# Linear attention and a mixture of experts on one core: 32-row inverses on GpSimd, and another order of the recurrence

## The chip, the core and the metric

One core of a Trainium2 chip runs the whole program in one launch. It has five engines with a queue each: PE (TensorE, matmuls), DVE (VectorE), ACT (ScalarE), POOL (GpSimd) and SP (SyncE, which only issues DMAs here). An engine takes its instructions in the order in which they were written and waits at each for what that one needs. The metric is the time of one execution in microseconds of the device, as the median of several runs.

## What is computed

The reference has three parts in a row, and all of it counts:

```
for t in range(768):                       # for each of 4 batches and 8 heads, state is 40x40
    y[t]  = r[t] @ state
    Sa    = state @ a[t]
    state = state * w[t] - outer(Sa, b[t]) + outer(v[t], k[t])
x   = rows of y, 3072 x 320
moe1: 8 experts, each row goes to its best one:  x = gate * (relu(x @ w1[e]) @ w2[e])
moe2: soft experts on 32 slots:  softmax over rows (dispatch) and over slots (combine)
```

## The kernel before, in words

**The attention stage** cuts the 768 steps into six chunks of 128. A chunk of one batch is a unit: 24 units, numbered u = 4 * chunk + batch, each with its 8 heads as four pairs. Within a unit the recurrence is turned into matmuls. The decays are multiplied up along the time axis by scans (P from the end, Q from the start); at L182 and bk at L174 and L184 are the inputs scaled by them; L206 and L223 form the lower triangles that say how a step acts on later ones (tiles lab and LAK). The 32 x 32 blocks on lab's diagonal have to be inverted, 32 heads and batches of a chunk and four blocks each. SP's DMAs gather them into the tile LD (gen_q); gen_t transposes LD on DVE (L257) so that each partition holds whole blocks, inverts two 16 x 16 halves by substitution, 15 steps of a product (L268) and a subtraction (L269), on DVE in chunk 0 and on POOL after that, and transposes back (L272, L275). gen_y then puts in the remaining 16 x 16 corner for each unit: 32 small matmuls (L284), an ACT copy (L287), 32 more (L292), a DVE subtraction (L295). gen_m uses the inverses: the two matmul groups L339 solve a unit's 128 rows in steps of 32, units k and k-1 together, with matmuls of zeros (L301) between. gen_a forms the outputs and the next state, gen_z turns them for the route and the next chunk. The route picks experts, scales the rows xt (L542, POOL) and scatters them by indirect DMA.

**The MoE stage** begins when the attention stage's banks are free, and keeps PE busy with L688, L706 and their like.

**The order** is written by hand. Each generator (d and c loads, e decays, k, b, q, x, t, y, m, a, z, r, and i and f for the initial memsets and the zero fills of two DRAM tables, issued on ACT's queue at L1189 and L1192) yields after a step, and the string SCHED (L1209) says by one letter at a time which generator takes its next step. Every engine's queue follows from it. PSUM has six banks in rotation (`bank`, L118) and two for gen_m. Weights for the MoE and the rest come by SP's queue.

The functions that the change touches:

Of the kernel before, what the change touches and what calls it, by code (L numbers as in the profile page):

```python
# [18 lines left out]
T = 128  # L19
NT = S // T  # L20
NP = 4
# [28 lines left out]


def blocks(a, o, dims):
    return bass.AP(a.tensor, a.offset + o, [list(a.ap[0]), [528, 2]] + dims)
# [16 lines left out]
def stage_attn(ctx, tc, la_d, vp_d, rz_d, vt_d, cst, rt):  # L70
# [19 lines left out]
    GB = [t[:, 0:H * (64 + D)].rearrange("t (h c) -> t h c", h=H) for t in gb_]  # L90
    GS = [per.tile([T, H, 32], F32, name=f"GS{i}") for i in range(2)]
    LAK = per.tile([T, H, T], F32, name="LAK")
# [10 lines left out]
    def load_first():  # L103
        pair = [RP, 2, NP, T]
        std = [pin.tile([RP, NP, T], F32, name=n, bufs=1 if i else 2) for i, n in enumerate(("lw", "lb", "la", "lk"))]
        lw1 = pin.tile([RP, NP, T], F32, name="lw", bufs=2)
        ba1, ba2 = (pt.tile(pair, F32, name="Tt", bufs=2) for x in range(2))
        ks = [t[:, 0:NP * T].rearrange("r (p t) -> r p t", p=NP) for t in gb_]
# [46 lines left out]
    def gen_e(u):  # L155
        lw = LA[u][0]
        At = AT[u] = pk.tile([RP, NP, T], F32, name="At", bufs=7)
        nc.scalar.activation(At, lw, AF.Relu, bias=lim[:, 0:1], scale=-1.0, accum_out=wf[:, 2 * u:2 * u + 1])
        nc.scalar.activation(At, lw, AF.Relu, bias=lim[:, 1:2], scale=1.0, accum_out=wf[:, 2 * u + 1:2 * u + 2])
        yield  # L160
        P = PT[u] = pk.tile([RP, NP, T + 1], F32, name="P", bufs=2)
        Q = QT[u] = pk.tile([RP, NP, T + 1], F32, name="Q", bufs=8)
        w = WE[u] = pk.tile([RP, NP, 1], F32, name="wend", bufs=10)
        nc.vector.memset(P[:, :, T:T + 1], 1.0)
        nc.vector.tensor_scalar(lw, lw, WLO, WHI, ALU.max, ALU.min)
        yield
        for p in range(NP):
            nc.vector.tensor_tensor_scan(rev(P[:, p, 0:T]), rev(lw[:, p, :]), one, 1.0, ALU.mult, ALU.mult)
            if p == 1:
                yield  # L170
        nc.vector.reciprocal(Q[:, :, 0:1], P[:, :, 0:1])  # L171
        yield
        bk = BK[u] = pl.tile([RP, NP, 2 * T], F32, name="bk", bufs=2)
        nc.gpsimd.tensor_tensor(ends(bk), LA[u][1].rearrange("r p (i s) -> r p i s", i=2),  # L174
                                P[:, :, 1:T + 1].rearrange("r p (i s) -> r p i s", i=2), ALU.mult)
        nc.gpsimd.tensor_copy(w, P[:, :, 0:1])
        yield
        for p in range(NP):
            nc.vector.tensor_tensor_scan(Q[:, p, 1:T + 1], lw[:, p, :], one, Q[:, p, 0:1], ALU.mult, ALU.mult)  # L179
            if p % 2:  # L180
                yield
        (nc.vector if u in (1, 3) else nc.gpsimd).tensor_tensor(At, LA[u][2], Q[:, :, 0:T], ALU.mult)  # L182
        yield
        nc.gpsimd.tensor_tensor(bk[:, :, 64:64 + T], LA[u][3], P[:, :, 1:T + 1], ALU.mult)  # L184
        yield

# [13 lines left out]
    def gen_b(u):  # L200
# [6 lines left out]
        yield  # L207
        lab = LAB[u] = pk.tile([T, H, T], F32, name="lab", bufs=7)
        if u == 0:
# [21 lines left out]
    def gen_q(u):  # L231
        tt, b = divmod(u, B)
        if b == 0:
            LD[tt] = pt.tile([T, B * H, 32], F32, name="Ld")
        for c in range(4):
            o = 32 * c
            nc.sync.dma_start(out=LD[tt][o:o + 32, b * H:(b + 1) * H, :], in_=LAB[u][o:o + 32, :, o:o + 32])
        yield
# [16 lines left out]
    def gen_t(tt):  # L255
        M = pt.tile([T, 32, 32], F32, name="Tm")
        nc.vector.transpose(out=M, in_=LD[tt].rearrange("p h t -> p t h"))  # L257
        yield
        eng = nc.gpsimd if tt else nc.vector
        eng.memset(blocks(VI, 0, [[32, 16], [1, 16]]), 0.0)  # L260
        eng.memset(blocks(VI, 0, [[33, 16]]), 1.0)
        tmp = pt.tile([T, 128], F32, name="Tx")
        yield
        for s in range(15):
            n, m = 15 - s, s + 1
            w = tmp[:, 0:2 * n * m].rearrange("p (k n m) -> p k n m", k=2, n=n)
            v = blocks(VI, 32 * (s + 1), [[32, n], [1, m]])
            eng.tensor_tensor(w, blocks(M, 33 * s + 32, [[32, n], [0, m]]), blocks(VI, 32 * s, [[0, n], [1, m]]), ALU.mult)  # L268
            eng.tensor_tensor(v, v, w, ALU.subtract)  # L269
            yield  # L270
        R = TT[tt] = pt.tile([T, B * H, 32], F32, name="Tt", bufs=2)
        nc.vector.transpose(out=R.rearrange("j h t -> j t h"), in_=VI)  # L272
        yield
        W = DT[tt] = pt.tile([T, B * H, 16], F32, name="Dt", bufs=1)
        nc.vector.transpose(out=W.rearrange("j h s -> j s h"), in_=VI[:, :, 0:16].rearrange("j t s -> j s t"))  # L275
        yield

    def gen_y(u):
        tt, b = divmod(u, B)
        R, gs = TT[tt][:, b * H:(b + 1) * H, :], GS[u % 2]  # L280
        ps = bank(T, H, 16)
# [165 lines left out]
    def gen_i():  # L447
# [10 lines left out]
        for i in range(2):  # L458
            nc.gpsimd.memset(GS[i], 0.0)
            nc.gpsimd.memset(RI[i][:, :, T:T + D], 0.0)  # L460
            for o in (0, 64):
                nc.gpsimd.tensor_copy(RI[i][o:o + D, :, T:T + D], eye[o:o + D, None, o:o + D].to_broadcast([D, NP, D]))
            yield
# [11 lines left out]
    def units(f, lo=0, by=1):  # L475
        for u in range(lo, U, by):
            yield from f(u)

    def routes():
        for tt in range(NT - 1):  # L480
# [3 lines left out]

    streams = dict(d=units(gen_d, B), c=units(gen_c), e=units(gen_e), k=units(gen_k), b=units(gen_b), q=units(gen_q),
                   x=units(gen_x), y=units(gen_y), m=(y for k in range(U + 1) for y in gen_m(k)), a=units(gen_a), z=units(gen_z),
                   t=(y for tt in range(NT) for y in gen_t(tt)), r=routes(), i=gen_i(), f=gen_f(), w=gen_w())
    load_first()
    for c in cst["sched"]:
        next(streams[c], None)  # L490
    for c in "idcekbqxtymazrf":
        for _ in streams[c]:
            pass


class Route:
# [9 lines left out]
    def run(self, tt, lg, xt, pp, tag, b0=0, b1=B):  # L506
# [34 lines left out]
        V.reciprocal(sm, sm)  # L541
        nc.gpsimd.tensor_tensor(xt[:, :, 1:XW], xt[:, :, 1:XW], sm.to_broadcast([T, n, DM]), ALU.mult)  # L542
        V.tensor_copy(xt[:, :, 0:1], cst["idm"][:, ti, None])
# [606 lines left out]
def program(tc, a, out_d):  # L1150
# [58 lines left out]
SCHED = (  # L1209
    "iicciieeiieieieeeffffdedidmmieeeeebbdeeeekecbbbbkkcbbkeekbkkbkebqbbxbebebxddebxbbbebbebqbxmeeebxxekebebbbekkkb"  # L1210
    "bbebbbqbxeeeebxexekbeebbkkdbbbbekebbbqbxeeeddddbxtxkbtbbbtbkktbbbbtbqbxkttttxtxttttttttteyeyyeeyydemyeymeeedmb"
    "dddmymebebkbemmbbbedkbemebbbqbeeedxdddmbexxembbbbkbmybeebmkemydbbeybqbxmeydmxbxdddmmabmaaabbbbmaaabaamebeccmbk"
    "amyamabkbqbeymaaamttcmaktmaztmaeztzatxaztzkaztxztxamazaaattmaccatamttytaaatyteecmtdkmmakkmazktzzzzmzyzemyzyemm"
    "ayeeedmmddadabeambebmaaekaaybmabbdbebmkccayaabbbqbexaeaaxxedeecbdddmbaazbbkzzmybbzzembzyzkebmmzeaebmabadabqbex"
    "aaeaaaxmxedacceaaedddmbaaabebbcbbbbaazbbmzezbqkmbzzxzmzkmzxkmykeemxykmedymakyemaaaerdemedddbaakabyamabbbemkacc"
    "yaambmbbaaabbbqbcmaazmzzttmzzxmzmztaextzmxataatmtaaaatamtyacctaayttmataamtmtctmatazemkzztmzdzkkmztzmakzmaeaaey"
    "aameyaaameedeyccbdddakabaybbbekbmbebaemamabbdbqbecxaazexmzzxemkzzmkzedzeeybdddmkbzebrmmmyakyaakkabbbaabaaamyba"
    "cacabebebqbedxeaeaaxxedeecbdddmbaazbbmyzezbbkzzebzbmeezybmzkbdybqbxmyemxxkmeymarkemdyaraaeedddbmbaayaaabbbmbka"
    "ccmbaaymembramababmbqbcmakazmezzxzttezmazzxdmazataexttmetaaktaaamktmacctaamtmtmataatmtctmatazmtzzetzzzrzmadmaa"
    "ameezaaaaacacbddadatbbbbbbbmaaabbbqbecexayaxzexkyzzeeyzzkkydzemkzymezmmyreedeybdddkbmmybbbbymebbmaebmkbeamaebq"  # L1220
    "aybdmxeaamexaaaxermdkamccyaeadddekbyaaabebbbbcbbaazbbmzezbqkzebzxmzekzdmxzxekmymaekrmaaaedymeedddbyaabaakabbmb"
    "bmacbcaamymebaaabbbqbcmakazmzzmezzttexmzmzadxzmxtaeaattemtaatkaaamktmatccaatmmtmtaaatmtctmataztmzzetzzrzzdmama"
    "aameezaaaaaabccadddatbbbbbybmabayaebbbqbecxeyaexazxymzedzmkezzyzzmerkkmzykerdyembydddembebkbymbbbbemabbekmeaam"
    "bqbayedxmaaeaaaxxdmeaccaamdmdeebkbmabaakbbbbmcebaazbbmzezbqmkebzzxezmzakemxazaaermxeaaaaambaccaabbbbbbbaaabbbq"
    "bckayakzymzttzmyzzmktzztmyzktymtkymtktrmxmamxaaaxmtaaaaatmtmrccataammtrmaaamcmaazmtzzzztztzmazttmaaamtaayaaamy"
    "yaccaaymaaammcmaazmzzmzzzyzmzmaymaaamaaaaamyaccaaymaaammcmaazzzmzzmzzzmymarymaaamaaaaamyaccaaymaammcmazzzmrzmz"
    "ymmaymazaarmaaaaaryaccaamymaammcmazzzmzmzzmmamaaamaaaaammaccaammaammazzzzzzmaraaaraaaaaaaarraaazzzzzzrrrr"
)
# [74 lines left out]
```

## Time and profile before

| | |
|---|---|
| time, median of 3 runs | 893.78 us (891.35 to 899.17) |
| the profiled execution | 880.59 us, of which the span is 878.6 us |
| PE / DVE / ACT / POOL busy | 780.0 / 483.9 / 363.4 / 234.0 us |
| first matmul of the MoE stage | 588 us |
| first use of a chunk's inverse, chunks 1 to 5 (L339) | 157.7, 232.8, 324.6, 409.7, 503.6 us |

The profile is one execution. Busy time is the time in which an engine works; waits are named by what ended them (`<-`). PEclk is the clock that TensorE was granted, as a share of full speed. Line numbers with an L are lines of the kernel above. The profiled execution is the fastest of those known of this kernel.

### The profile page before, as it was taken

What the parts mean: (1) busy time and instruction counts of PE and PEld (TensorE: products, weight loads), DVE (VectorE), ACT (ScalarE), POOL (GpSimd) and SP (SyncE); (2) the same over time, 40 slices, a digit from 0 to 9 for tenths busy, and PEclk for the clock granted to TensorE, in tenths of its full rate; (3) what the DMA queues carried; (4) which work ended last, traced back from release to release, by engine and by line L of the source; (5) the groups of instructions that cost most, each with busy time, mean ns of one, the idle gap of its engine ahead of it and who ended that gap; (6) DMA issues with size and microseconds to landing.
All of it is one profiled execution on the core that took longest, in us unless ns stands there. A gap on an engine that the chain in (4) does not pass through costs nothing. (4 is left out here: it accounts for less than half of the span.)

```text
span 878.6 us, 31034 instructions
## 1 busy us (share of the span) xinstructions
PE 780.0 (89%) x13468; PEld 661.4 (75%) x13468; DVE 483.9 (55%) x1334; ACT 363.4 (41%) x898; POOL 234.0 (27%) x404
## 2 busy tenths in 40 slices
PE   1385999999998987998999999979999999999894
PEld 1274888888877876887888687749999999999532
DVE  4378654665664674655373334355567666665423
ACT  1363553564653454544353131324444444443122
POOL 7131325223433543263225202020022012201210
PEclk9995598899996998998596798989999999999697
DMA  8822433443442343424231213345665567545755
GB/s 303 250 46 59 120 103 89 110 124 82 116 142 94 84 122 96 127 67 138 78 71 36 61 47 84 100 123 146 183 185 153 148 189 197 157 148 184 275 168 184
DMA packets 140627, 113.94 MB, mean 130 GB/s; under 512 B 64004, under 2 KB 118564, under 8 KB 140484
## 3 DMA queue, kind: packets, MB, share of 16 engines
q1 hardware_dynamic: 134304, 102.28, 41.2%
q10 hardware_dynamic: 3956, 5.09, 1.9%
q0 software_dynamic: 2224, 4.51, 1.5%
q8 instruction: 108, 1.77, 0.8%
q14 instruction: 35, 0.29, 0.1%
HBM read 95.73 MB, written 12.97 MB: 124 GB/s over the span
## 5 line engine op out<-in xcount | busy, mean ns | idle before, releaser
L784 POOL DMA_INDIRECT c_d<-cn,ix x32 | 34.2, 1068 | 218.0 <-DVE cn L781 202.1
L688 PE MATMUL psh<-xh,w1h 128*128 128x416 f32 x192 | 71.8, 374 | 0.0
L301 PE MATMUL psr<-zero 32*32 32x192 f32 x552 | 65.8, 356 | 2.2 <-issue 1.8
L690 ACT ACTIVATE hh<-psh 128x416 fp32r<-128x416 f32 x64 | 33.2, 519 | 81.5 <-PE psh L688 80.4
L174 POOL TENSOR_TENSOR bk<-lb,P 128x512 f32<-128x512 f32 x21 | 24.8, 1183 | 155.7 <-DVE Q L171 44.5
L692 DVE SCALAR_TENSOR_TENSOR hl<-psh,hh 128x416 fp32r<-128x416 f32 x64 | 37.8, 590 | 37.0 <-ACT hh L690 37.0
L344 ACT ACTIVATE GA<-psr 32x320 f32<-32x320 f32 x48 | 20.5, 428 | 85.2 <-PE psr L339 84.1
L328 PE MATMUL psr<-GA,lab 32*32 32x40 f32 (+1 forms) x768 | 51.8, 224 | 0.5 <-issue 0.5
L339 PE MATMUL psr<-Rs,Tt 32*32 32x40 f32 x1536 | 48.6, 214 | 1.7 <-issue 1.6
L395 PE MATMUL ps<-GA,KB 128*40 128x168 f32 (+1 forms) x384 | 48.2, 329 | 0.2 <-issue 0.2
L328 PEld LDWEIGHTS psr<-GA,lab 32*32 32x32 f32 (+1 forms) x768 | 45.2, 132 | 3.0 <-issue 1.0
L179 DVE TENSOR_TENSOR_SCAN Q<-lw,Q,one 128x128 f32<-128x128 f32 x88 | 47.1, 586 | 0.4
L706 PE MATMUL pso<-hh,w2h 128*128 128x416 f32 x128 | 45.4, 355 | 0.0
L206 PE MATMUL ps<-At,bk 64*128 64x128 f32 x384 | 38.3, 349 | 8.0 <-POOL bk L184 8.0
L688 PE MATMUL psh<-xl,w1h 128*128 128x416 f32 x128 | 45.3, 354 | 0.0
L688 PE MATMUL psh<-xh,w1l 128*128 128x416 f32 x128 | 45.1, 353 | 0.0
L707 PE MATMUL pso<-hh,w2l 128*128 128x416 f32 x128 | 44.8, 350 | 0.0
L398 DVE TENSOR_TENSOR yT<-ps,Q 104x256 f32<-104x256 f32 x48 | 20.2, 421 | 44.7 <-PE ps L395 44.3
L708 PE MATMUL pso<-hl,w2h 128*128 128x416 f32 x128 | 44.7, 350 | 0.0
L339 PEld LDWEIGHTS psr<-Rs,Tt 32*32 32x32 f32 x1536 | 41.6, 119 | 3.0 <-issue 2.8
L193 PE MATMUL ps<-kmask,bk 104*128 104x104 f32 x192 | 30.4, 295 | 15.1 <-ACT LAK L217 15.1
L212 ACT COPY lab<-ps 64x512 f32<-64x512 f32 x48 | 25.9, 580 | 43.4 <-PE ps L206 38.0
(272 smaller groups left out, 2114.8 us busy)
## 6 DMA issues: line engine op xcount, KB each, us to landing
r<-in_w SPq DMA_DIRECT2D x32, 320.0 KB
p<-in_p SPq DMA_DIRECT2D x16, 640.0 KB
r<-in_w SPq DMA_DIRECT2D x32, 256.0 KB
p<-in_p SPq DMA_DIRECT2D x8, 1024.0 KB
RI<-in_rz SPq DMA_DIRECT2D x24, 256.0 KB
vs<-in_vp SPq DMA_DIRECT2D x24, 256.0 KB
lw<-in_la SPq DMA_DIRECT2D x22, 256.0 KB
lb<-in_la SPq DMA_DIRECT2D x21, 256.0 KB
```

Of the source, the lines that this page charges most:

```text
L179: nc.vector.tensor_tensor_scan(Q[:, p, 1:T + 1], lw[:, p, :], one, Q[:, p, 0:1], ALU.mult, ALU.mult)
L206: nc.tensor.matmul(low[x][:, p, :], lhsT=bk[o:o + KP, p, 0:T], rhs=At[o:o + KP, p, :], start=True, stop=True)
L301: nc.tensor.matmul(bk[o:o + 32, DM:512], lhsT=z[i:i + 32, 0:32], rhs=z[i:i + 32, 0:512 - DM], start=False, stop=True, skip_group_check=Tru ...
L328: nc.tensor.matmul(R[o:o + n, h, :], lhsT=LAB[u][r:r + n, h, o:o + n], rhs=val(u, r // 32)[r:r + n, h, :], start=False, stop=True, skip_gr ...
L339: nc.tensor.matmul(R[o:o + 32, h, :], lhsT=TT[u // B][o:o + 32, u % B * H + h, :], rhs=Rs[o:o + 32, h, :], start=True, stop=True, skip_gro ...
L395: nc.tensor.matmul(ps[o:o + D, i, j:w], lhsT=KB[u][j // 64][:, 2 * p + x, :], rhs=G[:, 2 * p + x, :], start=False, stop=True, skip_group_c ...
L688: nc.tensor.matmul(ps, lhsT=l, rhs=r, start=(i == 0), stop=(i == len(ops) - 1))
L692: V.scalar_tensor_tensor(hl, ps, 0.0, hh.bitcast(F32), ALU.max, ALU.subtract)
L706: nc.tensor.matmul(o, lhsT=wh[:, c], rhs=hh, start=(f == 0), stop=False)
L707: nc.tensor.matmul(o, lhsT=wl[:, c], rhs=hh, start=False, stop=False)
L708: nc.tensor.matmul(o, lhsT=wh[:, c], rhs=hl, start=False, stop=(f == NF - 1))
L784: q = nc.gpsimd.indirect_dma_start(out=c_d[:], out_offset=bass.IndirectOffsetOnAxis(ap=ix[:, j:j + 1], axis=0), in_=cn[:, j, :], in_offset ...
```

## The change

Five things are different.

- The inverse of chunks 1 to 5 is one 32 x 32 substitution on POOL, 31 steps of a product (L289 after the change) and a subtraction (L290); gen_y is left for the four units of chunk 0. The result goes back into LD, which has two buffers, and the tile DT is there for chunk 0 only.
- The clamped decays are written to a PSUM bank (wc) and not over lw, and both kinds of scans read them there.
- The three products on POOL are a stream of their own, p; the copy of wend goes to ACT. At and lab have a buffer more.
- The scaling of xt in the route is four ACT instructions in place of one on POOL.
- SCHED is another string: the fills, the initial memsets and all the rest stand elsewhere.

```diff
+def diag(a):
+    ap = [list(x) for x in a.ap]
+    return bass.AP(a.tensor, a.offset, [ap[0], [33, 32]])
...
     def gen_e(u):
         lw = LA[u][0]
-        At = AT[u] = pk.tile([RP, NP, T], F32, name="At", bufs=7)
+        At = AT[u] = pk.tile([RP, NP, T], F32, name="At", bufs=8)
...
-        nc.vector.tensor_scalar(lw, lw, WLO, WHI, ALU.max, ALU.min)
+        wc = bank(RP, NP, T)
+        nc.vector.tensor_scalar(wc, lw, WLO, WHI, ALU.max, ALU.min)
         yield
         for p in range(NP):
-            nc.vector.tensor_tensor_scan(rev(P[:, p, 0:T]), rev(lw[:, p, :]), one, 1.0, ALU.mult, ALU.mult)
+            nc.vector.tensor_tensor_scan(rev(P[:, p, 0:T]), rev(wc[:, p, :]), one, 1.0, ALU.mult, ALU.mult)
...
+        for p in range(NP):
+            nc.vector.tensor_tensor_scan(Q[:, p, 1:T + 1], wc[:, p, :], one, Q[:, p, 0:1], ALU.mult, ALU.mult)
+            if p % 2:
+                yield
+
+    def gen_p(u):
+        P, At = PT[u], AT[u]
         bk = BK[u] = pl.tile([RP, NP, 2 * T], F32, name="bk", bufs=2)
         nc.gpsimd.tensor_tensor(ends(bk), LA[u][1].rearrange("r p (i s) -> r p i s", i=2),
                                 P[:, :, 1:T + 1].rearrange("r p (i s) -> r p i s", i=2), ALU.mult)
-        nc.gpsimd.tensor_copy(w, P[:, :, 0:1])
-        yield
...
+        nc.scalar.copy(WE[u], P[:, :, 0:1])
         yield
         nc.gpsimd.tensor_tensor(bk[:, :, 64:64 + T], LA[u][3], P[:, :, 1:T + 1], ALU.mult)
+        yield
+        (nc.vector if u in (1, 3) else nc.gpsimd).tensor_tensor(At, LA[u][2], QT[u][:, :, 0:T], ALU.mult)
...
         M = pt.tile([T, 32, 32], F32, name="Tm")
         nc.vector.transpose(out=M, in_=LD[tt].rearrange("p h t -> p t h"))
         yield
...
+        else:
+            nc.gpsimd.memset(VI, 0.0)
+            nc.gpsimd.memset(diag(VI), 1.0)
+            tmp = pt.tile([T, 512], F32, name="Tx")
+            yield
+            for s in range(31):
+                n, m = 31 - s, s + 1
+                w = tmp[:, 0:n * m].rearrange("p (n m) -> p n m", n=n)
+                v = VI[:, s + 1:32, 0:m]
+                nc.gpsimd.tensor_tensor(w, M[:, s + 1:32, s:s + 1].to_broadcast([T, n, m]), VI[:, s:s + 1, 0:m].to_broadcast([T, n, m]), ALU.mult)
+                nc.gpsimd.tensor_tensor(v, v, w, ALU.subtract)
+                yield
+        R = TT[tt] = LD[tt]
         nc.vector.transpose(out=R.rearrange("j h t -> j t h"), in_=VI)
...
-        nc.gpsimd.tensor_tensor(xt[:, :, 1:XW], xt[:, :, 1:XW], sm.to_broadcast([T, n, DM]), ALU.mult)
+        for j in range(n):
+            nc.scalar.mul(xt[:, j, 1:XW], xt[:, j, 1:XW], sm[:, j])
...
-    "iicciieeiieieieeeffffdedidmmieeeeebbdeeeekecbbbbkkcbbkeekbkkbkebqbbxbebebxddebxbbbebbebqbxmeeebxxekebebbbekkkb"
+    "eecceeeeeedeieeieeiiiipdpeeepdippipikebefemebdcfkkbkbfkkbbbbkbbibqkbbexbefpxxdbbbbpebbebepbbqbbepexbbpdebbbbbk"
```

What the order does is seen in three places. The first is the head of ACT's queue: the limit checks of the units' decays, the zero fills (xs and c_d) and the first evictions. Before:

```order
L158 ACTIVATE At,wf<-lw,lim 128x512
L159 ACTIVATE At,wf<-lw,lim 128x512
L1189 DMA xs<-zero 104x8x321
L1192 DMA c_d<-zero 128x256
L1189 DMA xs<-zero 104x8x321
L1192 DMA c_d<-zero 128x256
L1189 DMA xs<-zero 104x8x321
L1192 DMA c_d<-zero 128x256
L1189 DMA xs<-zero 104x8x321
L158 ACTIVATE At,wf<-lw,lim 128x512
L159 ACTIVATE At,wf<-lw,lim 128x512
L212 COPY lab<-ps 64x4x128 x2
```

After:

```order
L163 ACTIVATE At,wf<-lw,lim 128x512
L164 ACTIVATE At,wf<-lw,lim 128x512
L163 ACTIVATE At,wf<-lw,lim 128x512
L164 ACTIVATE At,wf<-lw,lim 128x512
L163 ACTIVATE At,wf<-xt,lim 128x512
L164 ACTIVATE At,wf<-xt,lim 128x512
L189 COPY wend<-P 128x4 x2
L1215 DMA xs<-zero 104x8x321
L1218 DMA c_d<-zero 128x256
L163 ACTIVATE At,wf<-xt,lim 128x512
L164 ACTIVATE At,wf<-xt,lim 128x512
L221 COPY lab<-ps 64x4x128
```

All seven fills stood ahead of the second unit's check; now three units' checks stand ahead of the first two fills, and the others come one by one after evictions.

The second is POOL's queue in the inverse of chunk 2 (Tm holds the blocks, VI the inverse). Before:

```order
L174 TENSOR_TENSOR bk<-lb,P 128x4x2x64
L176 COPY wend<-P 128x4
L182 TENSOR_TENSOR At<-la,Q 128x512
L184 TENSOR_TENSOR bk<-lk,P 128x4x128
L260 MEMSET VI 128x2x16x16
L261 MEMSET VI 128x32
L268 TENSOR_TENSOR Tx<-Tm,VI 128x30
L269 TENSOR_TENSOR VI<-VI,Tx 128x2x15
```

After, from the middle of the longer inverse:

```order
L289 TENSOR_TENSOR Tx<-Tm,VI 128x255
L290 TENSOR_TENSOR VI<-VI,Tx 128x17x15
L187 TENSOR_TENSOR bk<-lb,P 128x4x2x64
L191 TENSOR_TENSOR bk<-lk,P 128x4x128
L193 TENSOR_TENSOR At<-la,Q 128x512
L289 TENSOR_TENSOR Tx<-Tm,VI 128x256
L290 TENSOR_TENSOR VI<-VI,Tx 128x16x16
```

A unit's products stood ahead of the inverse; now those of two units stand between its steps.

The third is PE's queue up to the first use of chunk 2's inverse. Before:

```order
L365 MATMUL ps<-RI_121,vs 128x128 x8
L206 MATMUL ps<-At,bk 128x128 x8
L328 MATMUL psr<-GA_123,lab 64x40 x8
L292 MATMUL ps<-Tt,GS_130 32x16 x32
L376 MATMUL ps<-RI_121,vs 128x64 x8
L193 MATMUL ps<-kmask,bk 128x104 x4
L301 MATMUL psr<-zero 32x192 x2
L339 MATMUL psr<-Rs,Tt 32x40 x8
```

After:

```order
L257 MATMUL ps<-vt,LAK 64x40 x16
L440 MATMUL ps<-kmask,ST_115 104x104 x4
L448 MATMUL ps<-kmask,yT 128x104 x4
L215 MATMUL ps<-At,bk 128x128 x8
L327 MATMUL psr<-zero 32x192 x2
L365 MATMUL psr<-Rs,Ld 32x40 x8
```

L292 is gone, the inverse is read from Ld, and L257, L440 and L448 (a unit's value products, and the turning of states and outputs) stand ahead of the first use.

## Rows read from the trace of the kernel before

**Rows 1.** the page's part 1, busy time by engine.

```profile
PE 780.0 (89%) x13468; PEld 661.4 (75%) x13468; DVE 483.9 (55%) x1334; ACT 363.4 (41%) x898; POOL 234.0 (27%) x404
```

**Rows 2.** windows by stage: length, busy time (x instructions) by engine, PEclk, DMA share, GB/s.

```profile
0.00:33.00 33.00, 6.89 (x48) 5.98 (x48) 8.97 (x21) 4.47 (x10) 15.41 (x33) 1.00 0.90 296
33.00:89.30 56.30, 34.88 (x512) 31.32 (x512) 44.48 (x112) 27.25 (x68) 14.10 (x16) 0.80 0.32 83
89.30:157.70 68.40, 65.27 (x1528) 57.45 (x1524) 35.26 (x91) 32.38 (x84) 26.30 (x48) 0.77 0.36 100
157.70:232.80 75.10, 73.61 (x1975) 63.29 (x1973) 48.80 (x132) 42.30 (x113) 24.98 (x46) 0.99 0.42 109
232.80:324.60 91.80, 84.36 (x2030) 71.77 (x2029) 56.16 (x164) 43.90 (x118) 36.81 (x60) 0.91 0.41 111
324.60:409.70 85.10, 76.69 (x1914) 65.07 (x1915) 49.29 (x142) 39.29 (x105) 32.91 (x57) 0.92 0.38 102
409.70:503.60 93.90, 89.09 (x1838) 73.81 (x1836) 42.01 (x127) 34.91 (x93) 31.96 (x59) 0.73 0.27 73
503.60:588.00 84.40, 75.38 (x1744) 58.57 (x1742) 36.25 (x138) 24.13 (x65) 14.65 (x22) 0.94 0.29 78
588.00:814.00 226.00, 225.83 (x1509) 210.20 (x1510) 139.95 (x347) 101.40 (x211) 28.35 (x48) 0.99 0.60 170
```

**Rows 3.** windows again, by clock: the slow stretches and a clean one.

```profile
80.00:86.00 6.00, 0.04 (x4) 0.07 (x6) 5.59 (x14) 0.00 (x0) 0.00 (x0) 0.50 0.00 0
86.00:106.80 20.80, 19.97 (x453) 18.41 (x457) 12.23 (x36) 9.06 (x23) 7.38 (x8) 0.50 0.44 124
144.50:158.50 14.00, 14.00 (x310) 12.80 (x313) 5.96 (x16) 6.31 (x17) 3.63 (x4) 0.52 0.31 93
160.00:262.00 102.00, 98.34 (x2606) 84.73 (x2595) 65.65 (x186) 58.45 (x157) 35.33 (x56) 1.00 0.45 120
...
588.00:592.00 4.00, 3.83 (x19) 3.55 (x20) 2.42 (x8) 1.42 (x3) 0.00 (x0) 0.61 0.98 250
```

**Rows 4.** lines of PE, 158 to 264 us: busy, mean ns of one, idle before.

```profile
L284 PE MATMUL ps<-Dt,lab 32*32 32x16 f32 x384 | 4.4, 180 | 0.0
...
L292 PE MATMUL ps<-Tt,GS 32*32 32x16 f32 x320 | 3.8, 180 | 0.9 <-issue 0.9
```

**Rows 5.** POOL's timeline in chunk 1's inverse: start, length, what it ran.

```profile
128.47 0.25 POOL L268 TENSOR_TENSOR Tx<-Tm,VI 128x30 f32<-128x30 f32 x1 [15.31 <-DVE Tm L257]
...
134.75 0.43 POOL L268 TENSOR_TENSOR Tx<-Tm,VI 128x128 f32<-128x128 f32 x1
...
141.53 0.25 POOL L269 TENSOR_TENSOR VI<-VI,Tx 128x30 f32<-128x30 f32 x1
141.73 1.19 POOL L174 TENSOR_TENSOR bk<-lb,P 128x512 f32<-128x512 f32 x1
```

**Rows 6.** lines of DVE by form, the whole span.

```profile
L272 DVE STREAM_TRANSPOSE Tt<-VI 128x1024 f32<-128x1024 f32 x6 | 11.9, 1980 | 9.9 <-POOL VI L269 9.8
L257 DVE STREAM_TRANSPOSE Tm<-Ld 128x1024 f32<-128x1024 f32 x6 | 11.9, 1978 | 2.8 <-DMA Ld<-lab 2.4 <-issue 0.4
...
L268 DVE TENSOR_TENSOR Tx<-Tm,VI 128x128 f32<-128x128 f32 x1 | 0.3, 291 | 0.0
```

**Rows 7.** timelines of ACT (ACTq: its queue's DMA issues) and DVE, up to 36 us.

```profile
31.03 0.33 ACTq L1189 DMA_DIRECT2D xs<-zero  x1
31.41 0.72 ACT L158 ACTIVATE At<-lw,lim 128x512 f32<-128x512 f32 x1 [23.22 <-DMA GB<-in_la]
...
33.10 0.43 DVE L165 TENSOR_SCALAR lw<-lw 128x512 f32<-128x512 f32 x1 [18.59 <-ACT At L159]
```

**Rows 8.** DVE's timeline, two pairs of Q scans.

```profile
55.02 1.87 DVE L179 TENSOR_TENSOR_SCAN Q<-xt,Q,one 128x128 f32<-128x128 f32 x2
...
57.38 0.86 DVE L179 TENSOR_TENSOR_SCAN Q<-xt,Q,one 128x128 f32<-128x128 f32 x2
```

**Rows 9.** waits of PE over the span: us, times, longest.

```profile
PE ps L284 <- DVE Dt L275: 8.0, 1, 8.0
```

## What I expect, before the result

> **What bounds the kernel now.** I read the engines' shares first: PE is busy for 780.0 of 878.6 us and no other engine for more than 55% [rows 1]. Then the table of windows, cut where each chunk's inverse is first used (89.3, 157.7, 232.8, 324.6, 409.7 and 503.6 us) and where the MoE stage begins (588 us) [rows 2]. Three things stand there. From 588 to 814 us PE is busy in 225.83 of 226.00 us; the change touches nothing in that stage, which only starts earlier or later. Between 89 and 588 us PE is busy 89 to 98% of each row, but the granted clock is anywhere from 0.73 to 0.99: the attention stage is limited by PE's queue, and part of that by its clock. The first 89.3 us are another matter: PE works 41.8 us there, and DMA is 90% busy in the first 33 us.
>
> The clock goes between two levels [rows 3]: 1.00 from 160 to 262 us (2.4 GHz), 0.50 (1.2 GHz) elsewhere. After 140 us there are eight half-clock stretches, from 144.5 us to 588 us, 92.9 us together, 11.6 each, so 5.8 us lost in each. In 80 to 86 us PE does 0.04 us of work while it waits for DVE; the 20.8 us after that run at 0.50 with PE busy for 19.97 of them.
>
> **What goes from PE.** Each unit loses the 16-row correction: 32 matmuls L284 and 32 L292, for the 20 units of chunks 1 to 5. In the clean stretch six units' L284 take 4.4 us and five units' L292 3.8 us [rows 4], 0.73 and 0.76 us a unit, about 30 us over 20. PE's work in the new order, each matmul at its line's mean in that clean stretch, is 410 us for the attention stage against 439. (The same sum on the old order gives 75.5 us between the first uses of chunks 1 and 2, where the trace has 75.1 [rows 2].) The DVE and ACT pieces of it (L275, L287, L295) leave engines that are idle for a third or more of each row, and count for nothing.
>
> **What comes in its place: a longer inverse on POOL.** Chunk 1's L268/L269 pairs start at 128.47 us; the last ends at 141.78 [rows 5]. Thirty instructions in 13.3 us. The 30-element one takes 0.25 us, the 128-element one 0.43, and a product of 512 elements 1.19, with about 0.08 us between two: 0.277 us an instruction plus 1.93 ns an element. The change issues 62 of them over 2 x 5,456 elements: 17.2 + 21.1 = 38.2 us. Between them stand bk and At products of later units, 6, 6, 6, 9 and 0 in chunks 1 to 5, at 1.19 us each. With a DVE transposition on either side, 2.0 us each [rows 6], the path from LD to a usable inverse is 49.4, 49.4, 49.4, 53.0 and 42.3 us. POOL has the time: 25 to 37 us of 68 to 94 are busy now [rows 2].
>
> PE's work that the new order puts between that transposition and the inverse's first use is 43.5, 37.2, 38.2, 40.2 and 29.9 us. So PE reaches the first use early in every chunk, by 6, 12, 11, 13 and 12 us, and **waits**. Behind the waiting L365 its whole queue stands, the next unit's L202 and L215 too, so nothing fills the gap. I price a half-clock stretch of 11.6 us after each wait, 5.8 us lost, the mean above; at least 0, at most the 10.4 us that followed the wait at 80 us [rows 3].
>
> **The start.** ACT's queue now holds seven fill DMAs ahead of the second unit's limit check; the last is issued at 31.03, and the check starts at 31.41 us after 23.22 us of idleness; DVE's clamp waits for it, 18.59 us [rows 7]. In the new order the checks of units 0 to 2 stand ahead of the first fill. But the decays and the rest come over the same DMA engines, 90% busy, and fills of the same size must still go. Bounds: 0 (the data arrive no sooner), and 23 us, the whole idle stretch. I take 15, since the second and third units' decays are the first loads of their queue and only the later fills compete.
>
> **Clamp in PSUM.** The scans read one operand from PSUM. A pair of Q scans takes 1.87 us beside a running POOL product and 0.86 without [rows 8]. With POOL at work for 38 us a chunk this matters more than before, so I take the short time and give nothing for it. The Trainium skill ("SBUF — State Buffer", "SBUF: two separate sides") says that a DVE instruction with two SBUF inputs and a GpSimd one exclude each other; the rows agree with it, and by it the scans run free after the change. The price is one of six banks, held from the clamp to the last Q scan, in some units across a chunk's boundary. Below 0; above, each of 24 units stops PE for one pair of scans, 24 x 0.86 = 21 us. I take 4: in the clean stretch PE lacks 3.7 us of 102 with six banks [rows 3], and I grant as much again in one chunk's length.
>
> The rest is free: xt's scaling and the copy of wend go to ACT, which is idle for 40% or more of each row [rows 2], and the later memsets are due long after.
>
> **The sum.** Chunk 1's transposition began 2.0 us before 128.4. Less 15 at the start, and less 8.9 because PE has 48.0 us of work ahead of it in the new order and 56.9 in the old: 102.5. First use of chunk 1: 102.5 + 49.4 = 151.9 us (157.7 before). Then, each time, PE's work until the next transposition (31.5, 29.2, 27.0, 25.6), 5.8 for the clock, and the path: 238.6 (232.8), 323.0 (324.6), 408.8 (409.7), 482.5 (503.6). From the last first use to the MoE stage the trace takes 84.4 us for 65.3 us of work; the new order has 59.3, so 59.3 + 19.1 + 5.8: 566.7 us against 588. That is 21.3 us gained, 17 after the bank. The profiled execution took 880.59 us (span 878.6), 13.2 less than the median of the runs shown, 893.78; I carry the difference: 863.3 by the profile, **876.5** by the median.
>
> **The rivals.**
> A. *The waits cost no clock.* For it: the clean stretch has gaps and stays at 1.00. Against: the 6 us of idleness at 80 us stand inside a slow stretch. It gives back 5 x 5.8: 847.
> B. *The start gains nothing*, because DMA volume sets it. For: 90% busy, 296 GB/s in 33 us [rows 2]. Against: no load precedes a fill by need. 876.5 + 15 = 891.
> C. *Slower: the clock stays low from one wait to the next.* Every chunk now has an idle PE of 6 to 13 us, where the old order has one, 8.0 us at L284 [rows 9], and after that one the clock was half for over 20 us. PE's 25 to 31 us between first use and the next transposition are on the path, so all that is lost there counts. At 22 us of half clock a wait the loss is 11 instead of 5.8, which takes the forecast to 903, the point of no return; at 30 us it is 15: 876.5 + 5 x 9.2 = 922.
> D. *The scans still wait for POOL*: the clamp in PSUM doesn't do what it is for. Then two pairs a unit lose 1.0 us each; the four units ahead of a transposition lie on the path one after the other only in their last: 2 us a chunk, 10 in all: 886.
> E. *POOL is slower still on wide pieces.* The 128-element instruction takes 0.43 us on POOL and 0.29 on DVE [rows 5, 6], 1.48 times. At twice DVE's time 38.2 becomes 51.6 us, 13.4 a chunk on the path, 5 times: 943. Against it is the 512-element product, 1.19 us, that lies on the same line as the small ones. The Trainium skill ("GPSIMD Engine Reference", "4.1 Engine selection") speaks against the change: it puts elementwise work with two inputs on VectorE, GpSimd being about twice as slow. The trace has 1.48.
>
> **How the numbers follow.** A measurement here tells about 1% from no change: 884.8 and 902.7. Chances: forecast 0.45, A 0.14, B 0.19, C 0.14, D 0.05, E 0.03. The forecast's own range is 861 to 891 (15 us either way: 23 or 0 at the start, 3.8 us a chunk if POOL's price is off by a tenth), so four fifths of it are faster by over 1% and a fifth within. With A: faster 0.36 + 0.14 + half of D and a little of B, 0.54. Within 1%: 0.09 + 0.16 + 0.02, 0.27. Slower: C, E and the end of B, 0.19. The range takes A whole and C's beginning: 845 to 905.
>
> **What would show it.** In the profile of the changed kernel: the L289/L290 instructions of a chunk span some 38 us without the products between them, and the 512-wide product still takes 1.19; PE's longest waits are five at L365 on DVE's second transposition, 6 to 13 us each; the second unit's check starts before 15 us instead of 31; L310 and L318 appear for four units only; the scans take 0.40 to 0.46 us with no pairs of 1.8; POOL is busy some 340 us. If PE's waits at L365 are missing, the path on POOL is shorter than I think, or PE slower. If the waits are there and the first one ends at 165 us instead of 152, the start has failed. If the granted clock is under 0.75 in most rows between 150 and 560 us, C has come. A wait of PE on DVE's scans would mean that the bank costs more than 4 us.

## The result, and the profile after

| | before | changed |
|---|---|---|
| time, median of 20 runs each | 888.39 us (873.16 to 899.17) | 873.03 us (860.88 to 886.95) |
| the profiled execution | 880.59 us, span 878.6 | 870.97 us, span 869.1 |
| PE / DVE / ACT / POOL busy | 780.0 / 483.9 / 363.4 / 234.0 us | 753.3 / 461.5 / 368.5 / 321.8 us |
| first use of the inverse, chunks 0 to 5 | 89.3, 157.7, 232.8, 324.6, 409.7, 503.6 | 82.5, 160.7, 241.8, 327.2, 415.7, 493.5 |
| MoE stage begins | 588 | 580.5 |

The ratio is 0.986 (95% interval 0.982 to 0.990); by the medians 0.983, 15.4 us. The ratio with its interval is made from the runs within about 1.5% of each kernel's fastest, which favours a kernel whose times spread widely, so the ratio of the medians of all runs stands beside it below.

The windows of the changed kernel, cut at its transpositions (L266) and first uses (L365); columns as in [rows 2]:

```profile
33.00:82.50 49.50, 42.10 (x557) 37.77 (x558) 34.64 (x96) 26.39 (x70) 13.18 (x12) 1.00 0.54 135
...
110.00:160.70 50.70, 47.15 (x976) 39.41 (x976) 29.52 (x79) 21.51 (x62) 40.10 (x69) 0.90 0.32 90
160.70:194.10 33.40, 31.11 (x781) 26.96 (x784) 16.33 (x45) 20.76 (x55) 6.82 (x7) 1.00 0.53 139
194.10:241.80 47.70, 38.21 (x701) 31.23 (x689) 29.61 (x84) 23.79 (x65) 41.01 (x70) 0.95 0.30 82
241.80:279.30 37.50, 32.14 (x688) 27.47 (x688) 17.61 (x57) 17.88 (x47) 10.24 (x15) 0.86 0.47 127
279.30:327.20 47.90, 42.48 (x736) 34.47 (x737) 33.50 (x94) 23.55 (x66) 41.10 (x70) 0.89 0.34 94
327.20:364.80 37.60, 31.16 (x684) 26.52 (x684) 14.94 (x45) 18.25 (x48) 10.09 (x15) 0.88 0.38 99
364.80:415.70 50.90, 44.22 (x747) 36.32 (x744) 31.32 (x89) 24.31 (x67) 42.34 (x72) 0.89 0.42 118
415.70:452.40 36.70, 33.37 (x584) 28.53 (x580) 14.69 (x48) 15.18 (x42) 8.75 (x12) 0.69 0.25 59
452.40:493.50 41.10, 31.72 (x676) 25.43 (x672) 18.26 (x54) 12.02 (x33) 32.32 (x63) 0.99 0.21 53
493.50:580.50 87.00, 76.44 (x1330) 59.44 (x1330) 33.43 (x138) 27.35 (x72) 14.15 (x26) 0.81 0.29 80
580.50:806.50 226.00, 225.96 (x1509) 209.94 (x1510) 139.83 (x347) 101.23 (x211) 28.26 (x48) 0.99 0.60 169
```

From a transposition to the first use pass 50.7, 47.7, 47.9, 50.9 and 41.1 us, and POOL is busy for 40 to 42 of them (32 in the last). Between a first use and the next transposition POOL does 7 to 10 us of work, and PE, busy for 31 to 33 us of 33 to 38, sets the pace. The MoE stage is the same 226 us.

The inverse of chunk 2 in POOL's timeline, against [rows 5]:

```profile
196.25 0.25 POOL L289 TENSOR_TENSOR Tx<-Tm,VI 128x31 f32<-128x31 f32 x1 [11.35 <-DVE Tm L266]
...
214.09 1.17 POOL L187 TENSOR_TENSOR bk<-lb,P 128x512 f32<-128x512 f32 x1
215.22 1.18 POOL L191 TENSOR_TENSOR bk<-lk,P 128x512 f32<-128x512 f32 x1
216.36 1.17 POOL L193 TENSOR_TENSOR At<-la,Q 128x512 f32<-128x512 f32 x1
217.50 0.64 POOL L289 TENSOR_TENSOR Tx<-Tm,VI 128x256 f32<-128x256 f32 x1
218.22 0.73 POOL L290 TENSOR_TENSOR VI<-VI,Tx 128x256 f32<-128x256 f32 x1
...
239.49 0.25 POOL L290 TENSOR_TENSOR VI<-VI,Tx 128x31 f32<-128x31 f32 x1
```

43.5 us from the first to the last instruction, six products between them at 1.13 us a start: 36.7 us for the 62 instructions. The 256-element product takes 0.64 us, the subtraction 0.73.

PE's longest waits (us, times, longest), and then DVE's lines by form, to put beside [rows 8, 9]:

```profile
PE ps L202 <- POOL bk L191: 15.4, 1, 15.4
PE ps L232 <- ACT KB L205: 11.3, 1, 11.3
PE psr L365 <- DVE Ld L293: 10.4, 2, 5.5
PE psr L327 <- DVE Rs L357: 10.0, 14, 2.1
```

```profile
L180 DVE TENSOR_TENSOR_SCAN Q<-ps,Q,one 128x128 f32<-128x128 f32 x96 | 39.3, 463 | 0.6
...
L174 DVE TENSOR_TENSOR_SCAN P<-ps,one 128x128 f32<-128x128 f32 x96 | 33.9, 405 | 0.6
...
L171 DVE TENSOR_SCALAR ps<-lw 128x512 f32<-128x512 f32 x22 | 15.3, 696 | 0.1
```

For the inverse PE waits twice, 10.4 us in all. No scan pair is slow: 0.463 and 0.405 us a scan, none over 0.49, where a pair of L179 took up to 1.87 [rows 8]. The clamp itself takes 0.70 us, where one of before took 0.43 [rows 7].

ACT's timeline at the start, against [rows 7]:

```profile
8.64 0.71 ACT L163 ACTIVATE At<-lw,lim 128x512 f32<-128x512 f32 x1
...
13.04 0.57 ACTq L1215 DMA_DIRECT2D xs<-zero  x1
13.65 0.35 ACTq L1218 DMA_DIRECT2D c_d<-zero  x1
...
21.97 0.33 ACTq L1215 DMA_DIRECT2D xs<-zero  x1
31.94 0.33 ACTq L1218 DMA_DIRECT2D c_d<-zero  x1
32.31 0.42 ACT L205 COPY KB<-ps 128x320 f32<-128x320 f32 x1 [13.08 <-DMA vs<-in_vp]
```

The second unit's check starts at 8.64 us instead of 31.41. But ACT issues a fill at 21.97 us and nothing more until 31.94, when the next fill goes out, and the copy of KB behind it, for which PE waits 11.3 us, comes at 32.31.

### The profile page after: what moved, and what is told of

Read it like the earlier page. It is cut to its first block, busy times and chain, and to the rows that moved or that the text cites. A ratio compares the mean times of both kernels' runs of the same rounds, so it can differ in the third digit from the quotient of the medians.

```text
span 869.1 us, 26027 instructions
## 1 busy us (share of the span) xinstructions
PE 753.3 (87%) x10908; PEld 634.7 (73%) x10908; DVE 461.5 (53%) x1309; ACT 368.5 (42%) x926; POOL 321.8 (37%) x532
## 5 line engine op out<-in xcount | busy, mean ns | idle before, releaser
L289 POOL TENSOR_TENSOR Tx<-Tm,VI 128x31 f32<-128x31 f32 (+15 forms) x155 | 77.9, 502 | 55.1 <-DVE Tm L266 36.8
L290 POOL TENSOR_TENSOR VI<-VI,Tx 128x31 f32<-128x31 f32 (+15 forms) x155 | 83.5, 538 | 12.1
L327 PE MATMUL psr<-zero 32*32 32x192 f32 x552 | 68.2, 369 | 13.2 <-DVE Rs L357 10.0
L357 DVE TENSOR_TENSOR Rs<-psr,X 128x320 f32<-128x320 f32 (+1 forms) x50 | 24.4, 488 | 73.3 <-PE psr L354 69.5
L365 PE MATMUL psr<-Rs,Ld 32*32 32x40 f32 x1536 | 49.3, 217 | 12.4 <-DVE Ld L293 10.4
L591 POOL DMA_INDIRECT xs<-xt,rix x24 | 24.0, 1000 | 95.6 <-issue 67.1
L365 PEld LDWEIGHTS psr<-Rs,Ld 32*32 32x32 f32 x1536 | 42.3, 121 | 14.9 <-DVE Ld L293 11.5
L232 PE MATMUL ps<-At,bk 64*128 64x64 f32 x384 | 35.6, 325 | 13.2 <-ACT KB L205 11.3
L202 PE MATMUL ps<-kmask,bk 104*128 104x104 f32 x192 | 32.8, 312 | 15.7 <-POOL bk L191 15.4
```

Source lines behind the costliest of these rows:

```text
L232: nc.tensor.matmul(high[x][:, p, :], lhsT=bk[o:o + KP, p, T:2 * T], rhs=At[o:o + KP, p, 64:T], start=True, stop=True)
L289: nc.gpsimd.tensor_tensor(w, M[:, s + 1:32, s:s + 1].to_broadcast([T, n, m]), VI[:, s:s + 1, 0:m].to_broadcast([T, n, m]), ALU.mult)
L290: nc.gpsimd.tensor_tensor(v, v, w, ALU.subtract)
L327: nc.tensor.matmul(bk[o:o + 32, DM:512], lhsT=z[i:i + 32, 0:32], rhs=z[i:i + 32, 0:512 - DM], start=False, stop=True, skip_group_check=Tru ...
L365: nc.tensor.matmul(R[o:o + 32, h, :], lhsT=TT[u // B][o:o + 32, u % B * H + h, :], rhs=Rs[o:o + 32, h, :], start=True, stop=True, skip_gro ...
```

## The experiments

Twelve kernels were run, in three groups of four, each group on another chip; each is compared with the kernel before on its own chip. Its median there was 866.1, 886.5 and 888.4 us. The number behind a name is the order in which they were run: 1 to 4 are the first group, 5 to 8 the second, 9 to 12 the third. "Ratio" is to the kernel before, with its interval, then the ratio of medians. The changed kernel unedited was run in the second group only; in the other two, "over the changed kernel" compares ratios from different chips. Its expectation (experiment 5):

> The changed kernel itself, unedited, so that the others of this group have it on their own chip: the runs of the kernel before had a median of 866 us with the first experiments and 888 beside the changed kernel. If the gain does not depend on that, ratio 0.982 to 0.990.

Measured: 0.988 (0.980 to 0.995), medians 0.983: the gain came a second time, and 0.983 to 0.988 is what the others stand against.

### The start

**Fills back in front** (1). Edit: in SCHED of the changed kernel the four letters f go back ahead of the second unit's check:

```diff
-    "eecceeeeeedeieeieeiiiipdpeeepdippipikebefemebdcfkkbkbfkkbbbbkbbibqkbbexbefpxxdbbbbpebbebepbbqbbepexbbpdebbbbbk"
+    "eecceeeeffffeedeieeieeiiiipdpeeepdippipikebeemebdckkbkbkkbbbbkbbibqkbbexbepxxdbbbbpebbebepbbqbbepexbbpdebbbbbk"
```

> The changed kernel with its four steps of fills put back ahead of the second unit's limit check, as in the kernel before; nothing else moves. Theory S (the start gains what the profiles show): chunk 0's inverse is first used at 82.5 us in the changed kernel and at 89.3 before, so some 7 us of the gain are the start's: 880 us, ratio to the kernel before 0.993 to 0.996, chunk 0's first use near 89. The forecast's term: 15 us, 888, ratio 1.00. Rival (volume of DMA sets the start): no change, 873, ratio 0.986.

Measured: 1.0025 (0.995 to 1.010), medians 0.989. Chunk 0's inverse is first used at 87.6 us (here and below the start of the first L365 behind the chunk's second transposition) against 82.5 in the changed kernel:

```profile
87.58 0.78 PE L365 MATMUL psr<-Rs,Ld 32*32 32x40 f32 x9
```

By the medians 5 us of the 15 are the start's, by the ratio all of them.

**Fills moved in the kernel before** (7), f removed behind "ieee" and put back one by one, the first behind the second unit's check:

```diff
-    "iicciieeiieieieeeffffdedidmmieeeeebbdeeeekecbbbbkkcbbkeekbkkbkebqbbxbebebxddebxbbbebbebqbxmeeebxxekebebbbekkkb"
+    "iicciieeiieieieeededidmmieeefeebbdeeeekecbbbbfkfkcbbkeekbkkbkebqbbxbefbebxddebxbbbebbebqbxmeeebxxekebebbbekkkb"
```

> The kernel before with only the four steps of fills moved: behind the second unit's limit check and then one by one between the first units' steps, about where the changed kernel has them. Theory S: 7 us faster by the profiles, 14 by the first experiment's ratio: ratio 0.984 to 0.992, the second unit's check near 10 us instead of 31. If the whole gain of the change is the start, 0.986. Rival (the start is not on the path here): 1.00.

Measured: 0.979 (0.970 to 0.987), medians 0.994; its runs spread from 861 to 896 us. Chunk 0's first use: 83.5 us against 89.3. Again 5 us by the medians; by the ratio it would be 19, more than the whole change, which shows how far that number leans on a few runs when they spread so widely.

**Fills later still** (6): in the changed kernel the four letters stand behind chunk 0's second transposition, 40 letters apart:

```diff
-    "eecceeeeeedeieeieeiiiipdpeeepdippipikebefemebdcfkkbkbfkkbbbbkbbibqkbbexbefpxxdbbbbpebbebepbbqbbepexbbpdebbbbbk"
+    "eecceeeeeedeieeieeiiiipdpeeepdippipikebeemebdckkbkbkkbbbbkbbibqkbbexbepxxdbbbbpebbebepbbqbbepexbbpdebbbbbkbekp"
...
+    "kbxbqkebpppxkkkbbxkmbbcbbbbbbdbeqbededxebbpdpdedbextpxbbbbtttdtbtttttbtdbdtdtttbqtkkktxkxbbetfbxbtbbbbbbbbqyxm"
+    "eybyyeymyxekpymxkdepeepfdeedededyebbbxbkbpdbbmmybxbmmybmpbmqmkpdfdebkmbmkbbxmbbbbbbmybmbqmmmymattyttttttdfadaa"
```

> The changed kernel with its four steps of fills moved behind the inverse of chunk 0 (after 75 us), one by one. Theory S (fills compete with the first loads, and ACT stands behind their issue from 22 to 32 us while PE waits 11.3 us for a KB copy): that wait goes, chunk 0's first use comes at 70 to 76 us instead of 82.5, 7 to 12 us gained on the changed kernel, ratio 0.972 to 0.98. Rival (the loads themselves set the start, or the fills stop something later): ratio 0.986 or more.

Measured: 0.968 (0.962 to 0.975), medians 0.965, 855.6 us. That is 16 us faster than the changed kernel on the same chip. Its timeline of PE at chunk 0's first use:

```profile
65.31 0.78 PE L365 MATMUL psr<-Rs,Ld 32*32 32x40 f32 x9
```

That is 14 and 17 us earlier than in the two profiles of the changed kernel (79.7 and 82.5), and no wait for KB is among PE's long ones. So Theory S holds, and the change took about a third of what the fills cost: 89.3 to 82.5, where 65.3 was to be had. The 16 us are all the start's: from chunk 1's transposition to the MoE stage pass 468 us here, 470.5 and 471.5 in those two profiles.

### POOL's path and PE's work

**Half the inverse** (3; 16 of its 31 steps are left out):

```diff
             for s in range(31):
+                if s > 14:
+                    yield
+                    continue
```

> The changed kernel with 15 of the 31 steps of POOL's inverse left out in chunks 1 to 5 is not what runs here: 16 are left out, steps 15 to 30, so the inverse is not complete, and the path from transposition to first use is about 19 us shorter in each chunk. Theory P (POOL's path of 41 to 51 us paces every chunk, and PE's work of 189 us at full clock in the five stretches hides behind its 238): 25 to 48 us faster than the changed kernel, 825 to 848, ratio 0.93 to 0.96. Theory Q (PE paces; its waits at the first uses, 4.9, 0.7 and 5.5 us, are all that POOL costs): 11 us, 862, ratio 0.973.

Measured: 0.962 (0.954 to 0.970), medians 0.946. Against the changed kernel's ratio that is 2.6 to 3.8%, 22 to 33 us: Theory P, at its low end. On its own chip it is 38 us under the first experiment, which has its fills in front besides. The windows from transposition to first use of chunks 2 and 3:

```profile
191.00:236.20 45.20, 40.91 (x716) 33.12 (x704) 30.57 (x84) 23.81 (x65) 24.92 (x38) 0.93 0.34 96
269.50:312.10 42.60, 38.62 (x734) 32.02 (x737) 32.50 (x94) 23.68 (x66) 28.74 (x45) 0.99 0.48 140
```

POOL's load there falls from 41 to 25 and 29 us, and the stretch only from 48 to 45 and 43: now PE fills it, 41 of 45 us. POOL's path is only a few microseconds longer than PE's in a chunk, so shortening it alone soon meets PE.

**The correction's matmuls back on PE** (4): 64 of zeros, 32x32 by 16 columns, in the x step (L257).

```diff
+        if u >= B:
+            for h in range(2 * H):
+                for o in range(0, T, 32):
+                    nc.tensor.matmul(ps[o:o + 32, DM:DM + 16], lhsT=z[o:o + 32, 0:32], rhs=z[o:o + 32, 0:16],
+                                     start=True, stop=True, tile_position=(o, o))
```

> The changed kernel with 64 matmuls of zeros, 32x32 by 16 columns, added to the L257 step of each unit of chunks 1 to 5: the number and size that the correction took from PE, 1.5 us a unit, 30 us in all; the results do not depend on them. 12 of the 20 stand between a chunk's transposition and the first use of its inverse, 8 elsewhere. Theory P (POOL paces those stretches): only the 8 count, 12 us, 885, ratio 1.00. Theory Q (PE paces): 30 us less the 11 us of waits that it fills, at least 19, up to 30: 892 to 903, ratio 1.007 to 1.02.

Measured: 1.041 (1.032 to 1.050), medians 1.026: 4.3 to 5.3% over the changed kernel, 37 to 46 us for 31.4 us of PE's time. Neither theory allows more than the work itself, hence the next two. Part of the excess stands among PE's waits, ahead of the added matmuls, and is put down to nothing but their issue:

```profile
PE ps L261 <- issue: 7.2, 7, 1.7
```

**Only in the twelve covered units** (9), the same matmuls under another condition:

```diff
+        if u in (7, 8, 11, 12, 13, 15, 16, 17, 19, 20, 21, 23):
```

> The fourth experiment's 64 small matmuls of zeros, 1.5 us a unit, only in the 12 units whose L257 step stands between a transposition and the first use of the chunk's inverse (units 7, 8, 11 to 13, 15 to 17, 19 to 21, 23): 18 us of work. Theory P (POOL's path covers them): 0 to 5 us over the changed kernel, median over that of the kernel before 0.983 to 0.99, and the stretches from transposition to first use stay at 48, 48, 48, 51 and 41 us. Theory Q (PE paces): 18 us, 1.003. Theory K (the small matmuls bring the clock down, and a slow stretch reaches past the first use): 5 to 15 us, 0.99 to 1.00, with more half-clock time than in the changed kernel.

Measured: 1.001 (0.997 to 1.006), medians 0.996: 1.3 to 1.5%, 12 to 13 us for 18 us of covered work. P alone falls. K's range holds; Q's 18 us, 1.003, is over the ratio of medians but inside the interval of the other, so this run alone does not rule it out.

**The same time in wide matmuls** (10), in the same 20 units:

```diff
+        if u >= B:
+            for h in range(5):
+                nc.tensor.matmul(ps[:, DM:DM + 168], lhsT=z[:, 0:T], rhs=z[:, 0:168], start=True, stop=True)
```

> The same place as in the fourth experiment, all 20 units, but five matmuls of zeros over the whole array (128x128 by 168 columns) instead of 64 small ones: 1.6 us a unit at full clock, 32 us in all. The fourth experiment's kernel had 88 to 108 us of lost clock up to 600 us against 58 to 90 in the changed kernel, and 9 of its 13 slow stretches began just behind a group of the small ones. Theory K (small matmuls bring the clock down): the wide ones cost 8 units' worth, 10 to 18 us, ratio of medians 0.995 to 1.004, and no slow stretch begins behind them. Theory Q (work is work): as the small ones, ratio of medians 1.02 to 1.03.

Measured: 0.993 (0.989 to 0.998), medians 0.986: 0.3 to 0.7%, 3 to 6 us for 37.5 us of PE's time (340 ns each, overlapping; the trace has each of the 100 twice): even less than the 10 to 18 of K, and far from Q. The window of 100 to 560 us with the small ones in 20 units, in 12, with the wide ones, and then in the two profiles of the changed kernel:

```profile
100.00:560.00 460.00, 415.50 (x9836) 353.71 (x9836) 216.82 (x626) 195.15 (x529) 237.22 (x399) 0.85 0.32 86
```

```profile
100.00:560.00 460.00, 417.55 (x9419) 352.59 (x9413) 224.53 (x664) 201.06 (x545) 237.69 (x399) 0.87 0.33 87
```

```profile
100.00:560.00 460.00, 410.17 (x8130) 345.82 (x8126) 225.76 (x668) 201.46 (x547) 242.01 (x407) 0.94 0.35 92
```

```profile
100.00:560.00 460.00, 402.46 (x8042) 336.16 (x8042) 231.46 (x682) 203.33 (x554) 241.31 (x407) 0.89 0.34 93
```

```profile
100.00:560.00 460.00, 406.64 (x7996) 339.91 (x7994) 230.41 (x680) 202.93 (x552) 241.88 (x407) 0.87 0.34 91
```

PE is busy for 410 to 418 us in the first three; the granted clock is 0.85, 0.87 and 0.94, and 0.89 and 0.87 in the changed kernel. Over all runs of a kernel the mean clock is 0.882 (12 runs, small) and 0.915 (12 runs, wide) on one chip, and 0.883 (small) beside 0.909 (fills in front) on another; the changed kernel's own runs have 0.889 and 0.883. What is shown is the cost: 31 us of small matmuls cost more than their time, though POOL's path covers 18 of it, and on one chip 18 us of small ones end 9 us later, by the medians, than 37.5 us of wide ones (885.2 and 875.9). That the clock is the reason is not shown. With small ones in 20 units the clock is lower than with the fills in front on the same chip, but with small ones in 12 units it is hardly lower than the changed kernel's, and with wide ones it is higher: that wide matmuls raise the clock fits these rows as well as that small ones lower it, and the waits at issue are a cost of another kind.

**The wide inverse alone** (11), in the kernel before, gen_y kept for four units, SCHED untouched:

```diff
+        for s in range(31 if tt else 0):
+            n, m = 31 - s, s + 1
...
+            if s and s % 2 == 0:
+                yield
```

> The kernel before with only the wide inverse on POOL in chunks 1 to 5 and without the correction of its 20 units; the order is the old one (two of the 31 steps at a letter, three at the first). Theory P: the path from transposition to first use becomes 42 us at least (2.0 + 38.2 + 2.0) where the old order leaves PE 21 to 42 us of work; 25 to 40 us of waits at five first uses, less some 15 us of corrections that no longer stand on PE elsewhere: 10 to 35 us slower, ratio 1.01 to 1.04. Rival (what counts is PE's 36 us less): faster, ratio 0.97 to 0.98.

Measured: 1.095 (1.084 to 1.106), medians 1.099; 88 us slower, more than twice the upper end. The wait is not where I put it. PE's waits:

```profile
PE ps L211 <- POOL bk L189: 83.3, 6, 26.7
PE ps L419 <- ACT GA L394: 25.7, 1, 25.7
PE ps L438 <- DVE ST L427: 21.9, 4, 19.0
```

L211 is the first triangle of the next unit, and bk comes from POOL: in the old order the next unit's products stand behind the whole inverse, six waits, 83.3 us, where the kernel before has 8.0 at the same line. The new order puts products between the steps, and no such wait is left there once the start is past: PE waits for At at the same matmuls for 4.1 us in five pieces. That this is what makes the long inverse bearable fits both profiles; it was not tried by itself, and other matmuls moved too.

**At on DVE** (12), with the late fills:

```diff
-        (nc.vector if u in (1, 3) else nc.gpsimd).tensor_tensor(At, LA[u][2], QT[u][:, :, 0:T], ALU.mult)
+        (nc.vector if u in (1, 3, 8, 9, 12, 13, 16, 17, 18, 20, 21, 22) else nc.gpsimd).tensor_tensor(At, LA[u][2], QT[u][:, :, 0:T], ALU.mult)
```

> The kernel of the sixth experiment (fills behind chunk 0's inverse), and besides the At product (L193) of ten units that stands within POOL's inverse is done on DVE (0.67 us there, 1.18 on POOL): POOL's path is 2.4 us shorter in chunks 1 and 2 and 3.5 in chunks 3 and 4. Theory P: 5 to 10 us faster than the sixth, ratio to the kernel before 0.957 to 0.963. Rival (the product on DVE waits for POOL, or PE's clock sets those stretches as much): as the sixth, 0.965 to 0.97.

Measured: 0.972 (0.965 to 0.978), medians 0.966: as the sixth. Against the sixth the path shrank by 1.4, 0.5 and 2.0 us in chunks 2 to 4; PE's stretches between first use and transposition were 143.5 us in both kernels, and no more of the 5 to 10 us forecast came.

### The clamp

**In SBUF again** (2), in the changed kernel:

```diff
-        wc = bank(RP, NP, T)
+        wc = lw
```

> The changed kernel with the clamp in place in SBUF again, so that the scans read two SBUF operands beside POOL's longer inverse, and the six PSUM banks are free. Theory (the scans' port matters): scans beside POOL come in pairs of 1.8 us instead of 0.93, DVE busy grows by 20 to 40 us, and the time by 5 to 10 us: ratio 0.992 to 0.997. Rival (the bank costs more than the scans win): 4 us or more faster than the changed kernel, ratio 0.981 or less. Third: neither is on the path, ratio 0.986.

Measured: 1.028 (1.021 to 1.036), medians 1.010: 23 to 36 us over the changed kernel. DVE's lines:

```profile
L180 DVE TENSOR_TENSOR_SCAN Q<-lw,Q,one 128x128 f32<-128x128 f32 x88 | 60.7, 741 | 0.6
L174 DVE TENSOR_TENSOR_SCAN P<-lw,one 128x128 f32<-128x128 f32 x88 | 44.1, 551 | 0.6
```

0.741 and 0.551 us a scan where the changed kernel has 0.463 and 0.405, 37 us of DVE over the span, and chunk 1's path grows from 50.3 to 58.2 us. This is what the Trainium skill says ("SBUF — State Buffer", "SBUF: two separate sides"): a DVE instruction with two SBUF inputs and a GpSimd one that reads SBUF shut each other out, and with an operand in PSUM a scan has only one SBUF input. The runs agree, with 0.741 against 0.463 us a scan.

**In PSUM in the kernel before** (8), the scans reading wc too:

```diff
-        nc.vector.tensor_scalar(lw, lw, WLO, WHI, ALU.max, ALU.min)
+        wc = bank(RP, NP, T)
+        nc.vector.tensor_scalar(wc, lw, WLO, WHI, ALU.max, ALU.min)
```

> The kernel before with only the clamp written to a PSUM bank, held until the unit's last scan. Theory (scans beside POOL are what the bank buys, and the changed kernel without it was 4% slower because POOL works 38 us a chunk there, here 13): DVE busy falls by some 15 us, the time by 0 to 5: ratio 0.995 to 1.00. Rival (the bank's price, in an order that was not written for it): PE waits for banks, ratio 1.005 to 1.03.

Measured: 1.003 (0.997 to 1.009), medians 1.007: no gain, perhaps a small loss. DVE's busy time fell by 6 us, where some 15 were expected. That POOL's inverse takes only 13 us a chunk there, so that there is little to win, would explain it; no run separates the two.

## Why the prediction was right, step by step

The time, 876.5 forecast and 873.0 measured, and the gain, 17 and 15.4, agree better than the steps do; that they agree so well is in part luck.

- **PE ahead of chunk 1's transposition**: right, and in every profile. 8.9 us forecast; from chunk 0's transposition to chunk 1's pass 56.1 us before (70.2 to 126.4) and 48.0 now (62.0 to 110.0). The other profiles of the old order (experiments 7, 8 and 11) have 59.9, 61.9 and 61.8 there, the seven others of the new one without added matmuls on the way 48.0 to 49.9.
- **POOL's path**: right. 49.4, 49.4, 49.4, 53.0, 42.3 forecast; 50.3, 47.6, 47.9, 50.9, 41.1 measured from the start of one transposition to the end of the other. Rival E fell: nothing is slower on wide pieces. (POOL's busy time came to 321.8 us, where some 340 were expected.)
- **The start**: the term was mis-sized, 15 us for 7 (10 in the second profile); chunk 1's first use came at 160.7 us, between the 152 forecast and the 165 that was to mean that the start had failed. What failed is "only the later fills compete": the new places are still within the loads, and ACT itself stands at a fill for 9.6 us. The bound of 23 was about right for fills that are out of the way (65.3 against 89.3).
- **PE's waits**: wrong. Five of 6 to 13 us, 54 in all, were forecast; three came, 4.9, 0.7 and 5.5. I had costed PE's work up to the first use at full clock; it ran at 0.89 to 0.95 in four of the five windows, with PE busy for 38 to 47 us in them. PE still stands idle for 34.5 us of the five stretches, but 11 of it at the first use and the rest in short waits ahead of it. So the waits changed their place, not the end: POOL's path sets those stretches either way, though the third experiment shows that it does so by a few microseconds only.
- **The clock**: 5.8 us behind each wait was about the size here, with a cause that stays open. The stretches from first use to transposition took 33.4, 37.5, 37.6 and 36.7 us, 145 in all, where 136.5 were forecast (113.3 of work and four times 5.8); the tail 87.0 for 84.2. Chunk 4's has no wait for the inverse ahead of it and the lowest clock, 0.69. In the first experiment's profile, on another chip, the same four took 123.6. The 5.8 was misread besides: the trace of before has eleven half-clock stretches from 144.5 to 588 us and not eight, 106 us together and 9.6 each, which makes it 4.8. Rival C did not come: of the rows between 150 and 560 us only chunk 4's is under 0.75, and the mean clock of the changed kernel's runs is 0.883 on the second group's chip, that of the kernel before 0.892.
- **PE's 30 us**: taken for time alone. The fourth and tenth experiments show that such small matmuls can cost more than their time, which the sum left out. What their removal gave back in the change itself is not separated from what the longer stretches without it took.
- **The bank**: 4 us were charged. No wait for a bank stands among PE's longest; the eighth experiment has 2 to 6 us in the old order, within its interval. Rival D fell: no scan took over 0.49 us.

By the profile the MoE stage begins at 580.5 us, where 566.7 was worked out: 7.5 us of the 14 are there at chunk 1's transposition, the rest are PE's slower stretches less POOL's shorter path. That the median still came out within 4 us is luck: the profiled execution of before was 7.8 us faster than the median of its 20 runs, that of the changed kernel 2.1, and I had carried over 13.2. By the profiles alone 863.3 was forecast and 871.0 measured, a gain of 9.6 for 17.

What stays open is how the 15 us divide. By the medians both tests of the start give 5 us, and chunk 0's first use agrees (6 to 10 us between profiles), so some 10 are left for the rest; by the ratios the start is all of it. The 8 us between the first two transpositions would make up most of that rest, and they come back in every profile; they were not tried by themselves. From chunk 1's transposition to the MoE stage, where the long inverse runs, the profiles disagree: 462 us before and 470.5 and 471.5 in the changed kernel, but 481 and 476 in the seventh and eighth experiments, which keep the old inverse and ran on the same chip as the 471.5, in profiled executions of 896 and 895 us. That is anything from 9 us lost to 10 gained: whether the long inverse, the change's largest piece, pays by itself is not shown.

## What to carry to other kernels

Zero fills and other writes that nobody needs soon should be issued when the first loads are through; the best version here is the changed kernel with its fills later (0.968). Here ACT, for which others wait, stood at their issue; another queue was not tried. A long inverse on a slow engine holds up whatever stands behind it in that engine's queue: 83.3 us of PE's waits in the old order. Work of many small matmuls should not be priced by its busy time alone: here 31 us of it cost 37 to 46, and 37.5 us of wide ones 3 to 6.

## What was not expected of the hardware

With 37.5 us of wide matmuls of zeros added, the granted clock of 100 to 560 us was 0.94 and the cost 3 to 6 us; with 31.4 us of 32x32 ones it was 0.85, and without either 0.89 and 0.87. PE's busy time was nearly the same, 402 to 416 us of 460, so the mean busy time of such a window does not tell its clock. The Trainium skill ("TensorE: Matmul & The Clock Gate", "What's actually happening") has the gate follow how busy the engine has been recently; means over 460 us neither bear that out nor speak against it. What the chip counts, no run here shows.
